# One DMA for both heads' keys and queries, and the first expert weights one unit earlier

## The chip, the cores and the metric

The kernel runs on one core of a Trainium2 chip. The metric is the device time of one execution in microseconds (us). Five engines work side by side, each through its own queue in order: PE (matmuls and transposes), DVE (elementwise work and reductions), ACT (activations and copies), POOL (elementwise work) and SP, which here only issues the DMA transfers.

## The reference

Three layers follow each other: attention, a mixture layer with one expert, and one with four.

```python
# q, k, v: (2, 8, 576, 64), f32
q_d, k_d, v_d = (t.reshape(B, H, 144, 4, D).mean(3) for t in (q, k, v))
out_up = np.repeat(softmax(q_d @ k_d.T / 8) @ v_d, 4, axis=2)     # pooled attention
scores = np.where(np.abs(i - j) < 4, q @ k.T / 8, -1e9)           # local band
out = out_up + softmax(scores) @ v
x = out.transpose(0, 2, 1, 3).reshape(1152, 512)
x = (s * np.maximum(x @ w_in, 0) ** 2 + b) @ w_out                # 512 -> 2048 -> 512
p = probs / (probs.sum(-1, keepdims=True) + 1e-9)
y = sum(p[:, e:e+1] * (np.maximum(x @ w1[e], 0) @ w2[e]) for e in range(4))   # 512 -> 1024 -> 512
```

The weights `w_in` and `w_out` of the first layer arrive as 64-bit floats, read as pairs of 32-bit words.

## The kernel before

**Attention** is cut into 16 units. Unit u covers two heads (j = u mod 4) and one of four groups of tokens (two batches, each in halves of 256 and 320 queries). The units go through a software pipeline of eight steps: iteration i runs `a_step` of unit i (transposes of keys and queries, `kT`, `qz`, `qd`), `k_step` (pooled keys, on POOL), `b_step` of unit i-1 (scores, maxima `ml` and `md`, exponentials `pl` and `pd`), `norm_step` and `v_step` of i-1, `c_step` of i-2 (transposes of the probabilities), `d_step` of i-3 (values, `ud`, `xg`) and `x_step` of i-3 (the unit's columns of x, in two parts: ACT writes the high part, POOL the low one, L717 and L719). Keys are loaded only for the first half of a batch (units 0 to 3 and 8 to 11), queries for each unit, both two iterations ahead (`load_k`, `load_q`).

**The weights** stream through `load_next`, one piece of 1 MB at a time into the pool `raw` with two buffers. A piece of the first layer is converted by `prep` in six steps: ACT takes the magnitude (L157), DVE clamps it (L161), joins the words (L167 and L175) and puts the sign on (L186), ACT makes the high part (L196), DVE the low part (L199). The last step also calls `load_next` for the next piece. The steps wait in the list `side`; `side_step` takes one, four times in an iteration. The first layer's first block has four pieces, called c0 to c3 here: c0 and c1 hold `w_in`, c2 and c3 `w_out`. The next block's first two, c4 and c5, follow. Products of the first block (L316, `psm`) are put between the attention's steps: those on x for the first group of tokens add up unit by unit.

**What sets the order.** The program is written as a list of steps, and a scheduler of the framework sets each engine's order from it, except on POOL, where the order is as written. On the chip each engine runs its queue in that order, so an instruction that waits holds up all behind it. SP issues the transfers in its own order, and a transfer waits there for its buffer and for one of eight completion counters, each of which is used again by the eighth transfer after it.

Of the kernel before, what the change touches and what calls it, by code (L numbers as in the profile page):

```python
# [8 lines left out]
F32 = mybir.dt.float32  # L9
# [13 lines left out]
def attn_moe_moe_kernel(  # L23
# [14 lines left out]
    nc = tc.nc  # L38
    B, H, S, D = q.shape
# [4 lines left out]
    TQ = 64  # L44
# [6 lines left out]
    FAC = 4  # L51
    SD = S // FAC
    ND = SD // 2
    KP = 96
    KR = S // KP
# [44 lines left out]
    def load_next():  # L100
        if not stream:
            return
        n, which, half = stream.pop(0)
        wi, wo, f0 = blocks[n]
        m = 2 if n < n_moe1 else 1
        dt = I32 if n < n_moe1 else F32
        if n < n_moe1:
            wi, wo = wi.bitcast(I32), wo.bitcast(I32)
        f0 += half * 256
        if which == 0:  # L110
            src = wi[:, f0 * m : (f0 + 256) * m].rearrange("(k p) f -> p k f", p=P)
        else:
            src = wo[f0 : f0 + 256, :].rearrange("(c p) d -> p c d", p=P)
        if n < n_moe1:
            t = rawp.tile([P, 2048], dt, tag="raw", name="raw")
        else:
            if "raw2" not in pools:
                t = rawp.tile([P, 2048], dt, tag="raw", name="raw2")
                pools["raw2"] = [t[:, :1024], t[:, 1024:]]
            t = pools["raw2"].pop(0)  # L120
            pools["raw2"].append(t)
        nc.sync.dma_start(out=t.rearrange("p (a b) -> p a b", a=src.shape[1]), in_=src)
        raw[n, which, half] = t
# [205 lines left out]
    def make_mask(t, m):  # L329
        if t == 0:  # L330
            nc.gpsimd.memset(mask, 0.0)
        off = t * TQ - window(t) if t <= MX else S - TQ - window(NTQ - 1)
        for sgn in (1, -1):
            nc.gpsimd.affine_select(
                out=mask[:, t : t + m],
                in_=mask[:, t : t + m],
                compare_op=ALU.is_ge,
                fill=NEG,
                base=FAC - 1 + sgn * off,
                pattern=[[0, m], [-sgn, W]],  # L340
                channel_multiplier=sgn,
            )
# [7 lines left out]
    def keep_warm(ps, c0, m):  # L350
        for _ in range(m if c0 < 448 else 0):
            nc.tensor.matmul(  # L352
                ps[:, c0:], idle[:, :P], idle[:, : 512 - c0], start=True, stop=True
            )
# [11 lines left out]
    def norm_probs():  # L366
        nc.vector.tensor_reduce(out=prs, in_=pr, axis=AX.X, op=ALU.add)
        nc.vector.tensor_scalar(out=prs, in0=prs, scalar1=1e-9, scalar2=None, op0=ALU.add)
        nc.vector.reciprocal(out=prs, in_=prs)
        nc.vector.tensor_tensor(  # L370
            out=pr, in0=pr, in1=prs.to_broadcast([P, NT // P, E]), op=ALU.mult
        )
# [7 lines left out]
    ap4 = rctx.enter_context(tc.tile_pool(name="att4", bufs=1, side="right"))  # L380
# [15 lines left out]
    def unit(u):  # L396
        g, j = divmod(u, NP)
        b, hf = divmod(g, HALVES)
        return g, j, b, hf

    def tiles(hf):

        return (0, CUT) if hf == 0 else (CUT, NTQ - CUT)
# [6 lines left out]
    def bank():  # L410
        return psa.tile([P, 512], F32, tag="a", name="psa")
# [14 lines left out]
    def load_k(u):  # L426
        if u < NU and unit(u)[3] == 0:
            g, j, b, hf = unit(u)
            kn = ap4.tile([KP, KR, 2, D], F32, tag="kn", name="kn", bufs=2)
            for a in range(2):  # L430
                nc.sync.dma_start(
                    out=kn[:, :, a], in_=k[b, 2 * j + a].rearrange("(p r) d -> p r d", r=KR)
                )
            loaded["k", u] = kn

    def load_q(u):
        if u < NU:
            g, j, b, hf = unit(u)
            n0, m = tiles(hf)
            gd = m * TQ // FAC  # L440
            qn = ap2.tile([MX * TQ // FAC, FAC, 2, D], F32, tag="qn", name="qn")
            for a in range(2):
                nc.sync.dma_start(
                    out=qn[:gd, :, a],
                    in_=q[b, 2 * j + a, n0 * TQ : (n0 + m) * TQ, :].rearrange(
                        "(n r) d -> n r d", r=FAC
                    ),
                )
            loaded["q", u] = qn

    def load_v(u):
# [494 lines left out]
    def l1_steps(n, g):  # L946
        hs = hidden[n, g] = []
        if n < n_moe1:
            return [lambda fc=fc: moe1_l1(n, g, fc, hs) for fc in range(FC)]

        def run(half, i):
            if i == 0:
                hidden["steps"] = moe2_l1(n, g, half, hs)
            hidden["steps"][i]()

        return [lambda half=half, i=i: run(half, i) for half in range(2) for i in range(4)]

    def l2_steps(n, g):
        if n < n_moe1:
            return [lambda dc=dc: moe1_l2(n, g, dc, hidden[n, g]) for dc in range(KD)]  # L960
        t0, m = PARTS[g]
        return [
            lambda i=i: moe2_l2(n, t0 // P + i, i * P, hidden[n, g]) for i in range(2 * m // P)
        ]
# [6 lines left out]


    load_k(0)
    load_q(0)
    make_mask(0, 1)
    make_mask(1, CUT - 1)
    load_k(1)
    load_q(1)
    keep_warm(bank(), 0, 8)
    pool_order = ExitStack()  # L980
    pool_order.enter_context(tc.manual_schedule(engines={mybir.EngineType.Pool}))
# [12 lines left out]
    for i in range(last + 1):  # L994
        if i == 1:
            make_mask(CUT, 2)
            make_mask(MX + 1, 1)
        if i == 2:
            side += prep(0, 0, 0) + prep(0, 0, 1) + prep(0, 1, 0) + prep(0, 1, 1)
        if i == NU - 1:  # L1000
            norm_probs()
        if i == NU - NP:
            rctx.close()
            pools["wx"] = ctx.enter_context(
                tc.tile_pool(name="wx", bufs=1, side="right", reuse_waits="tile")
            )
            side += prep(1, 0, 0) + prep(1, 0, 1)
        for f, lag in steps:
            u = i - lag
            if 0 <= u < NU:  # L1010

                with tc.high_priority(30) if f is a_step and u < NP else nullcontext():
                    f(u)
            if f is x_step and u >= 0 and u % NP == NP - 1:
                slots += l1_steps(0, u // NP) + l2_steps(0, u // NP)
                if u < NP:

                    for _ in range(3):
                        slots.pop(0)()
            if f in (k_step, c_step) and slots and i < last:  # L1020
                slots.pop(0)()
            if f in (b_step, k_step, c_step, v_step):
                side_step()
        load_k(i + 2)
        load_q(i + 2)
        load_v4(i)
        load_v(i)
        if i == 4:
            load_small()
        if i < 2:  # L1030
            load_next()
    pool_order.close()
    while len(slots) > 4:
# [100 lines left out]
```

## Time and profile before

| | us |
|---|---|
| median of 3 runs | 708.98 |
| lowest and highest | 701.22, 710.42 |
| the profiled execution: its time | 706.03 |
| its span on the core | 704.2 |
| PE busy in the span | 690.5 (98%) |
| DVE, ACT, POOL busy | 417.0, 341.6, 105.0 |

The attention and the first block lie in the first 154 us; behind them the products follow without a gap. Busy time of PE counts matmuls at either granted clock. The page gives the clock in tenths of full speed (2.4 GHz): 1.00 is that, 0.50 is 1.2 GHz.

### The profile page before, as it was taken

Reading aid. Unit: us, or ns where it says so; the run is one execution under the profiler, and the core shown is the slowest. Engines: PE = TensorE matmul, PEld = TensorE weight load, DVE = VectorE, ACT = ScalarE, POOL = GpSimd, SP = SyncE. Lnnn points to the kernel's source line nnn. Section 1 sums busy time; section 2 is a strip of 40 time slices with the busy share of each in tenths; the row PEclk is TensorE's granted clock in tenths of the full one; section 3 lists DMA queues with packets and bytes.
Section 4 is the critical chain, followed back from the end, with each engine's and each line's share of the span. In section 5 each row is a group of like instructions: output and inputs, shape, how many; then the busy total and the mean of one; then the engine's idle time right before and its main releaser. Section 6 shows DMA issues by size and latency. Waiting matters only on the chain.

```text
span 704.2 us, 11441 instructions
## 1 busy us (share of the span) xinstructions
PE 690.5 (98%) x4496; PEld 629.8 (89%) x4496; DVE 417.0 (59%) x759; ACT 341.6 (49%) x830; POOL 105.0 (15%) x128
## 2 busy tenths in 40 slices
PE   8799999999999999999999999999999999999997
PEld 5678888899999999999899898899898998998996
DVE  3898848869893532578443645645645556365442
ACT  3666646768695655775443424324324234233220
POOL 5320353010000200103011111201210212010000
PEclk9979959999999999999999999999999999999999
DMA  8764625323350000100120200202201112021012
GB/s 183 192 175 95 118 61 139 114 84 118 122 179 1 1 31 1 61 1 31 30 60 31 61 31 31 89 2 59 61 30 60 31 31 70 21 61 31 1 58 77
DMA packets 54549, 46.40 MB, mean 66 GB/s; under 512 B 32608, under 2 KB 43104, under 8 KB 54496
## 3 DMA queue, kind: packets, MB, share of 16 engines
q1 hardware_dynamic: 54496, 45.67, 23.3%
q8 instruction: 35, 0.57, 0.3%
q14 instruction: 18, 0.15, 0.1%
HBM read 43.31 MB, written 2.36 MB: 65 GB/s over the span
## 4 chain that ended last, share of the span: by engine, by line
PE 89%; DVE 6%; ACT 2%; DMA 1%; issue 1%; POOL 1%; SPq 0%; ACTq 0%; POOLq 0%; DVEq 0%
PE psm L316 42%; PE psx L867 25%; PE psx L316 13%; PE psa L600 2%; PE psa L688 2%; PE psa L660 2%; DMA kn<-in_k_dram 1%; PE psa L618 1%; PE psa L681 1%; PE psa L512 1%; PE psa L494 1%; DVE cv L175 1%; DVE cv L161 0%; PE psa L352 0%; ACT cv L157 0%
## 5 line engine op out<-in xcount | busy, mean ns | idle before, releaser
L316 PE MATMUL psm<-w,h 128*128 128x512 f32 x864 | 208.7, 391 | 0.0
L316 PEld LDWEIGHTS psm<-w,h 128*128 128x128 f32 x864 | 158.5, 188 | 30.0
L867 PE MATMUL psx<-x,w 128*128 128x320 f32 (+1 forms) x768 | 117.7, 296 | 0.0
L867 PEld LDWEIGHTS psx<-x,w 128*128 128x128 f32 x768 | 109.2, 189 | 1.7
L259 POOL TENSOR_TENSOR sw<-raw 128x256 f32<-128x256 f32 x32 | 30.4, 971 | 407.5 <-DMA raw<-in_moe_w_dram 268.7
L882 ACT COPY r<-psx 128x320 f32<-128x320 f32 (+1 forms) x96 | 38.0, 396 | 92.7 <-PE psx L867 92.5
L885 ACT ACTIVATE h<-r 128x320 fp32r<-128x320 f32 (+1 forms) x96 | 42.1, 444 | 83.8 <-DVE r L896 83.8
L938 DVE SCALAR_TENSOR_TENSOR acc<-psm,pr,acc 128x512 f32<-128x512 f32 x63 | 47.2, 749 | 57.8 <-PE psm L316 57.8
L867 PE MATMUL psx<-t,w 128*128 128x320 f32 (+1 forms) x448 | 80.2, 302 | 0.2 <-DVE r L896 0.2
L316 PE MATMUL psm<-x,w 128*128 128x320 f32 (+2 forms) x420 | 74.4, 325 | 4.2 <-ACT x L717 3.3
L896 DVE TENSOR_TENSOR r<-psx,r 128x320 f32<-128x320 f32 (+1 forms) x96 | 43.2, 456 | 59.0 <-PE psx L867 57.1
L316 PEld LDWEIGHTS psm<-x,w 128*128 128x128 f32 x420 | 66.7, 199 | 6.8 <-ACT x L717 3.8
L867 PEld LDWEIGHTS psx<-t,w 128*128 128x128 f32 x448 | 67.0, 188 | 4.5 <-DVE r L896 0.5
L886 DVE SCALAR_TENSOR_TENSOR h<-r,h 128x320 fp32r<-128x320 f32 (+1 forms) x96 | 47.6, 501 | 18.5 <-ACT h L885 16.4
L316 PE MATMUL psm<-h,w 128*128 128x256 f32 (+2 forms) x360 | 58.0, 306 | 0.0
L316 PE MATMUL psx<-h,w 128*128 128x384 f32 (+1 forms) x312 | 55.9, 327 | 0.0
L316 PEld LDWEIGHTS psm<-h,w 128*128 128x128 f32 x360 | 51.0, 189 | 1.9 <-issue 1.3
L316 PEld LDWEIGHTS psx<-h,w 128*128 128x128 f32 x312 | 52.0, 188 | 0.0
L316 PE MATMUL psx<-x,w 128*128 128x384 f32 (+2 forms) x252 | 43.1, 320 | 0.0
L316 PEld LDWEIGHTS psx<-x,w 128*128 128x128 f32 x252 | 40.6, 188 | 0.0
L237 DVE TENSOR_TENSOR w<-raw,w 128x1024 fp32r<-128x1024 f32 x16 | 19.5, 1224 | 25.4 <-ACT w L234 25.4
L784 DVE TENSOR_TENSOR h<-r,h 128x384 fp32r<-128x384 f32 (+2 forms) x40 | 21.6, 541 | 19.7 <-ACT h L783 18.4
(109 smaller groups left out, 894.1 us busy)
## 6 DMA issues: line engine op xcount, KB each, us to landing
raw<-in_moe_w_dram SPq DMA_DIRECT2D x32, 512.0 KB
raw<-in_moe_w_in_dram SPq DMA_DIRECT2D x8, 1024.0 KB
raw<-in_moe_w_out_dram SPq DMA_DIRECT2D x8, 1024.0 KB
kn<-in_k_dram SPq DMA_DIRECT2D x16, 144.0 KB
v<-in_v_dram SPq DMA_DIRECT2D x8, 288.0 KB
out_dram<-acc SPq DMA_DIRECT2D x9, 256.0 KB
qn<-in_q_dram SPq DMA_DIRECT2D x16, 80.0 KB
vn<-in_v_dram SPq DMA_DIRECT2D x16, 72.0 KB
```

What stands on the lines that cost most here:

```text
L237: nc.vector.tensor_tensor(out=k0[1], in0=source(), in1=f32(k0[0]), op=ALU.subtract)
L259: nc.gpsimd.tensor_tensor(out=operand(out), in0=operand(x), in1=operand(y), op=op)
L316: nc.tensor.matmul(o, stat(ps, kk), mov(pm, kk, i), start=c == 0, stop=c == len(terms) - 1)
L600: nc.tensor.matmul(ps[0][:, t * W : t * W + W], qz[:, t].rearrange("p a q -> p (a q)"), kT[:, k0 : k0 + W], start=False, stop=t == m - 1,)
L660: nc.tensor.transpose(ps[:W, n : n + width], x, ident[:width, :width])
L784: nc.vector.tensor_tensor(out=h[1], in0=r, in1=f32(h[0]), op=ALU.subtract)
L867: nc.tensor.matmul(ps, s_ap(n, half, a, w, kk), xt[x, pi][b][:, kk], start=first and c == 0, stop=c == len(terms) - 1, skip_group_check=True,)
L882: nc.scalar.copy(t, st[name])
L885: nc.scalar.activation(out=h[0][:, halves[hf]], in_=t, func=ACTF.Relu)
L886: nc.vector.scalar_tensor_tensor(out=h[1][:, halves[hf]], in0=t, scalar=0.0, in1=f32(h[0][:, halves[hf]]), op0=ALU.max, op1=ALU.subtract,)
L896: nc.vector.tensor_tensor(out=st[t], in0=st[name], in1=st[t], op=ALU.add)
L938: nc.vector.scalar_tensor_tensor(out=a, in0=ps, scalar=p_e, in1=a, op0=ALU.mult, op1=ALU.add)
```

## The change

Each pair of transfers for the two heads' keys becomes one, and so does each pair for the queries; the keys get a third buffer. The first piece of the weights is issued before the loop, behind the keys and queries of units 0 and 1 and ahead of those of unit 2; the second at the end of iteration 0, where the first was; the third and later ones come, as before, when a piece is converted. The conversion starts in iteration 1 in place of iteration 2.

```diff
--- before.py
+++ after.py
@@ -426,11 +426,10 @@
     def load_k(u):
         if u < NU and unit(u)[3] == 0:
             g, j, b, hf = unit(u)
-            kn = ap4.tile([KP, KR, 2, D], F32, tag="kn", name="kn", bufs=2)
-            for a in range(2):
-                nc.sync.dma_start(
-                    out=kn[:, :, a], in_=k[b, 2 * j + a].rearrange("(p r) d -> p r d", r=KR)
-                )
+            kn = ap4.tile([KP, KR, 2, D], F32, tag="kn", name="kn", bufs=3)
+            nc.sync.dma_start(
+                out=kn, in_=k[b, 2 * j : 2 * j + 2].rearrange("a (p r) d -> p r a d", r=KR)
+            )
             loaded["k", u] = kn
 
     def load_q(u):
@@ -439,13 +438,12 @@
             n0, m = tiles(hf)
             gd = m * TQ // FAC
             qn = ap2.tile([MX * TQ // FAC, FAC, 2, D], F32, tag="qn", name="qn")
-            for a in range(2):
-                nc.sync.dma_start(
-                    out=qn[:gd, :, a],
-                    in_=q[b, 2 * j + a, n0 * TQ : (n0 + m) * TQ, :].rearrange(
-                        "(n r) d -> n r d", r=FAC
-                    ),
-                )
+            nc.sync.dma_start(
+                out=qn[:gd],
+                in_=q[b, 2 * j : 2 * j + 2, n0 * TQ : (n0 + m) * TQ, :].rearrange(
+                    "a (n r) d -> n r a d", r=FAC
+                ),
+            )
             loaded["q", u] = qn
 
     def load_v(u):
@@ -976,6 +974,7 @@
     make_mask(1, CUT - 1)
     load_k(1)
     load_q(1)
+    load_next()
     keep_warm(bank(), 0, 8)
     pool_order = ExitStack()
     pool_order.enter_context(tc.manual_schedule(engines={mybir.EngineType.Pool}))
@@ -995,7 +994,7 @@
         if i == 1:
             make_mask(CUT, 2)
             make_mask(MX + 1, 1)
-        if i == 2:
+        if i == 1:
             side += prep(0, 0, 0) + prep(0, 0, 1) + prep(0, 1, 0) + prep(0, 1, 1)
         if i == NU - 1:
             norm_probs()
@@ -1027,7 +1026,7 @@
         load_v(i)
         if i == 4:
             load_small()
-        if i < 2:
+        if i == 0:
             load_next()
     pool_order.close()
     while len(slots) > 4:
```

How this moves instructions is seen on two engines. **SP, from its first transfer on** (kn is a unit's keys, qn its queries, v4 and vn its values, raw a piece of the weights). Before:

```order
L431 DMA kn_118<-in_k_dram 96x6x64 x2
L443 DMA qn_121<-in_q_dram 64x4x64 x2
L431 DMA kn_137<-in_k_dram 96x6x64 x2
L443 DMA qn_140<-in_q_dram 64x4x64 x2
L418 DMA v4_196<-in_v_dram 72x4x256
L458 DMA vn_198<-in_v_dram 72x2x64
L431 DMA kn_190<-in_k_dram 96x6x64 x2
L443 DMA qn_193<-in_q_dram 64x4x64 x2
L465 DMA vn_198<-in_v_dram 72x3x64 x2
L122 DMA raw_202<-in_moe_w_in_dram 128x4x512
```

Now:

```order
L430 DMA kn_118<-in_k_dram 96x12x64
L441 DMA qn_120<-in_q_dram 64x8x64
L430 DMA kn_135<-in_k_dram 96x12x64
L441 DMA qn_137<-in_q_dram 64x8x64
L122 DMA raw_139<-in_moe_w_in_dram 128x4x512
L430 DMA kn_188<-in_k_dram 96x12x64
L441 DMA qn_190<-in_q_dram 64x8x64
L418 DMA v4_192<-in_v_dram 72x4x256
L456 DMA vn_194<-in_v_dram 72x2x64
L463 DMA vn_194<-in_v_dram 72x3x64 x2
L122 DMA raw_198<-in_moe_w_in_dram 128x4x512
```

The 16 transfers ahead of the first piece of the weights have become four, and the keys and queries of unit 2 stand behind that piece; the second piece, which stood behind unit 3's loads, stands ahead of them.

**DVE, units 0 and 1** (ml and md are negated maxima, qz and qd a unit's queries, cv the piece in conversion). Before, from unit 0's `ml` to unit 1's `pl` scaling there is no conversion:

```order
L608 TENSOR_REDUCE ml_217<-psa_220 128x4
L526 TENSOR_SCALAR qz1_109<-psa_253 64x4x64
L620 TENSOR_REDUCE md_219<-psa_220 128x1
L533 TENSOR_REDUCE qd1_111<-psa_253 64x64 x2
L608 TENSOR_REDUCE ml_300<-psa_303 128x4
L633 TENSOR_SCALAR sum0_106<-sum0_106 128x7
L634 RECIPROCAL sum0_106<-sum0_106 128x7
L635 TENSOR_TENSOR pl_216<-pl_216,sum0_106 128x288
```

Now the first piece stands between, its first step ahead of unit 0's `ml`:

```order
L606 TENSOR_REDUCE ml_221<-psa_224 128x4
L524 TENSOR_SCALAR qz1_109<-psa_259 64x4x64
L531 TENSOR_REDUCE qd1_111<-psa_259 64x64
L618 TENSOR_REDUCE md_223<-psa_224 128x1
L531 TENSOR_REDUCE qd1_111<-psa_259 64x64
L167 TENSOR_SCALAR cv_238<-cv_238 128x1024
L175 SCALAR_TENSOR_TENSOR cv_238<-raw_139,cv_238 128x1024
L631 TENSOR_SCALAR sum0_106<-sum0_106 128x7
L606 TENSOR_REDUCE ml_298<-psa_301 128x4
L632 RECIPROCAL sum0_106<-sum0_106 128x7
L186 SCALAR_TENSOR_TENSOR cv_238<-raw_139,cv_238 128x1024
L633 TENSOR_TENSOR pl_220<-pl_220,sum0_106 128x288
```

**DVE, from unit 8's maxima to `xg` of unit 6** (cv_1431 and cv_1552 are c4 and c5 in the program before, cv_1529 is c5 in the new one). Before:

```order
L175 SCALAR_TENSOR_TENSOR cv_1431<-raw_819,cv_1431 128x1024
L161 TENSOR_SCALAR cv_1552<-cv_1552 128x1024
L186 SCALAR_TENSOR_TENSOR cv_1431<-raw_819,cv_1431 128x1024
L633 TENSOR_SCALAR sum0_106<-sum0_106 128x7
L167 TENSOR_SCALAR cv_1552<-cv_1552 128x1024
L634 RECIPROCAL sum0_106<-sum0_106 128x7
L175 SCALAR_TENSOR_TENSOR cv_1552<-raw_927,cv_1552 128x1024
L526 TENSOR_SCALAR qz1_109<-psa_1108 64x4x64
L533 TENSOR_REDUCE qd1_111<-psa_1108 64x64 x2
L697 TENSOR_SCALAR ud_1150<-psa_1135 128x80
L635 TENSOR_TENSOR pl_1079<-pl_1079,sum0_106 128x288
L705 TENSOR_TENSOR xg_1152<-psa_1135,ud_1150 128x320
```

Now:

```order
L175 SCALAR_TENSOR_TENSOR cv_1529<-raw_814,cv_1529 128x1024
L633 TENSOR_TENSOR pl_936<-pl_936,sum1_107 128x360
L636 TENSOR_TENSOR pd_938<-pd_938,sum1_107 80x288
L618 TENSOR_REDUCE md_1064<-psa_1065 128x1
L524 TENSOR_SCALAR qz1_109<-psa_1090 64x4x64
L531 TENSOR_REDUCE qd1_111<-psa_1090 64x64 x2
L695 TENSOR_SCALAR ud_1132<-psa_1117 128x80
L199 TENSOR_TENSOR w01_1388<-cv_1409,w00_1387 128x1024
L703 TENSOR_TENSOR xg_1134<-psa_1117,ud_1132 128x320
```

Between unit 8's `md` and unit 9's `qz` stood five steps of conversion, and none now; one step of c5 stands ahead of unit 7's scaling, and the low part of c4 (L199) has come ahead of `xg`.

## Rows read from the trace of the kernel before

**Rows 1.** Windows by stage: busy us of each engine (instructions), PEclk, DMA share, GB/s.

```profile
0.00:22.00 22.00, 18.68 (x125) 13.04 (x126) 9.42 (x28) 10.10 (x33) 10.20 (x26) 1.00 0.87 191
22.00:46.00 24.00, 20.94 (x184) 16.48 (x181) 21.76 (x38) 14.43 (x51) 9.77 (x10) 0.86 0.73 179
290.00:704.00 414.00, 410.10 (x2447) 372.77 (x2445) 222.60 (x394) 155.63 (x339) 51.12 (x57) 1.00 0.13 41
```

**Rows 2.** Windows: the three stretches at the lower granted clock.

```profile
31.90:38.70 6.80, 6.80 (x48) 5.43 (x48) 4.80 (x8) 3.97 (x14) 1.80 (x2) 0.50 0.50 107
48.90:55.60 6.70, 6.70 (x49) 5.92 (x48) 4.88 (x15) 4.44 (x19) 0.78 (x1) 0.50 0.93 233
86.30:103.50 17.20, 16.02 (x83) 13.93 (x84) 9.13 (x23) 6.94 (x30) 8.69 (x8) 0.50 0.26 58
```

**Rows 3.** Waits of PE, 0 to 140 us: total us, times, longest.

```profile
PE psm L316 <- ACT x L717: 3.3, 2, 2.0
```

**Rows 4.** Timeline of SP's DMA queue: start, us, what [idle before].

```profile
0.74 1.38 SPq L431 DMA_DIRECT2D kn<-in_k_dram  x2
...
6.15 0.60 SPq L418 DMA_DIRECT2D v<-in_v_dram  x1
...
11.00 0.41 SPq L122 DMA_DIRECT2D raw<-in_moe_w_in_dram  x1
```

**Rows 5.** DMA issues of the page: sizes of one load.

```profile
raw<-in_moe_w_in_dram SPq DMA_DIRECT2D x8, 1024.0 KB
...
kn<-in_k_dram SPq DMA_DIRECT2D x16, 144.0 KB
```

**Rows 6.** Chain that ended last, its first loads: start, us, what.

```profile
1.51 3.63 DMA kn<-in_k_dram
...
7.94 4.09 DMA kn<-in_k_dram
```

**Rows 7.** Windows: the DMA engines while small pieces, then while large ones are moved.

```profile
2.00:8.00 6.00, 5.44 (x32) 2.89 (x31) 0.52 (x2) 1.25 (x4) 2.20 (x6) 1.00 0.68 152
13.00:16.00 3.00, 3.00 (x22) 2.32 (x21) 0.89 (x3) 2.37 (x12) 0.35 (x2) 1.00 1.01 351
```

**Rows 8.** Timeline of ACT: start, us, what [idle before <- releaser].

```profile
11.81 0.38 ACT L524 ACTIVATE qz<-psa 64x256 f32<-64x256 f32 x1 [1.98 <-PE psa L352]
...
19.70 1.14 ACT L157 ACTIVATE cv<-raw 128x1024 f32<-128x1024 f32 x1
```

**Rows 9.** Timeline of DVE, 11 to 30 us.

```profile
11.42 0.46 DVE L608 TENSOR_REDUCE ml<-psa 128x4 f32<-128x288 f32 x1 [1.99 <-PE psa L600]
...
16.23 0.46 DVE L608 TENSOR_REDUCE ml<-psa 128x4 f32<-128x288 f32 x1 [2.33 <-PE psa L600]
...
28.73 1.22 DVE L199 TENSOR_TENSOR w<-cv,w 128x1024 fp32r<-128x1024 f32 x1
29.87 0.42 DVE L705 TENSOR_TENSOR xg<-psa,ud 128x256 f32<-128x256 f32 x1
```

**Rows 10.** Timeline of DVE: L161 twice.

```profile
33.94 0.69 DVE L161 TENSOR_SCALAR cv<-cv 128x1024 f32<-128x1024 f32 x1 [1.88 <-ACT cv L157]
...
42.40 1.45 DVE L161 TENSOR_SCALAR cv<-cv 128x1024 f32<-128x1024 f32 x1
```

**Rows 11.** Timeline of POOL, 41 us.

```profile
41.03 2.26 POOL L474 TENSOR_TENSOR v<-v 72x512 f32<-72x512 f32 x1
```

**Rows 12.** Timeline of PE, 47 us.

```profile
46.83 1.34 PE L600 MATMUL psa<-kT,qz 128*128 128x72 f32 x10 [0.68 <-DVE qz L526]
```

**Rows 13.** Timeline of DVE, 78 to 86 us.

```profile
78.74 1.21 DVE L175 SCALAR_TENSOR_TENSOR cv<-raw,cv 128x1024 int32<-128x1024 int32 x1
...
82.40 1.57 DVE L175 SCALAR_TENSOR_TENSOR cv<-raw,cv 128x1024 int32<-128x1024 int32 x1
...
85.35 0.24 DVE L697 TENSOR_SCALAR ud<-psa 128x80 f32<-128x80 f32 x1
```

**Rows 14.** Timeline of PE, 87 us.

```profile
86.90 0.90 PE L316 MATMUL psm<-x,w 128*128 128x320 f32 x2 [1.31 <-ACT x L717]
```

## The prediction

> **What bounds the kernel now.** I read the busy time by stage first. From 290 us on, PE is busy 410.1 of 414 us [rows 1], and the products look the same from 154 us; no edit touches an instruction there, so what can change lies in the first 154 us. In the first 22 us DVE is busy for only 9.4 us and POOL for 10.2; from 22 to 46 us DVE is busy 21.8 of 24 and PE 20.9 [rows 1]: the reader is to see DVE as the pace there and PE behind it.
>
> Second, the granted clock. It is 0.50, the 1.2 GHz level, in three stretches: 6.8, 6.7 and 17.2 us long [rows 2]. PE is busy throughout the first two and 16.0 us of the third, so at full clock that work would take 3.4, 3.4 and 8.0 us less. What PE did before each: it had waited 0.68 us for unit 5's queries at 46.8 us, two us before the second [rows 12], and 1.31 us for x of unit 6 until 86.9, where the third begins [rows 14]. The waits for x on ACT come to 3.3 us, two in number, the longest 2.0 [rows 3]: so the other is that of 2.0, and it ends where unit 0's x is written (its `xg` at 29.87 [rows 9]), just ahead of the first stretch.
>
> Third, SP's queue and the chain: the chain begins with keys that land (3.63 us from 1.51, 4.09 from 7.94 [rows 6]), and SP issues without a pause, two loads in 1.38 us at the start, up to the first piece of the weights at 11.00 [rows 4].
>
> **The change, part by part** (against the profiled execution, 706.0 us, 2.9 below the median of the runs, 709.0).
>
> *One load for two.* Unit 0's keys: now the second half starts at 1.51 and takes 3.63, landed at 5.14 [rows 6]. With one load the first bytes go 0.77 us earlier (issue at 0.74), but the other 144 KB follow in the same transfer [rows 5]; at 152 GB/s and a busy share of 0.68 [rows 7] the engines' full rate for these pieces is 152/0.68 = 224 GB/s (estimate), so 0.66 us. Gain between 0 (issue takes as long as two) and 0.77; the values' load, one transfer of the same 288 KB, is issued in 0.60 us [rows 4], nearer to one than to two, so I take 0.3, below the middle because the bytes stay. Later merged loads shorten SP's queue, which is not what is waited for after 20 us: nothing.
> The Trainium skill (DMA: Bandwidth & Descriptors, Anatomy of one DMA) fits a transfer as about 2.0 us plus its bytes at 436 GB/s; by that the merged keys would land near 4.0 and gain 1.1 us (estimate). The trace disagrees: by the same fit 144 KB take 2.3 us, and 3.63 were measured [rows 6].
>
> *The first piece ahead of unit 2's keys.* SP's four loads end about 3.4 us (four of 0.6 to 0.7), and the piece follows. Bytes ahead of it: 2 x 288 + 2 x 128 KB (unit 0's and 1's queries are 64 KB each half, by 64 rows of 1 KB) = 0.85 MB, 3.8 us at 224 GB/s from 2.0; then 1.05 MB at 351 GB/s [rows 7], 3.0 us: landed at 8.8. If SP needs as long for a merged load as for two, the issue is at 6.15 and it lands 5 us later, as it does now (issued 11.00, the fast bytes over at 16 [rows 4, 7]): 11.2. I take 10. Unit 2's keys, 0.30 MB, come 1.3 us behind: 10.1 to 12.5 against 12.03 now [rows 6]. Cost 0 (from -0.2 to +0.5): they are wanted no sooner than unit 1's `qz`, at 11.81 [rows 8].
>
> *The conversion in units 0 and 1.* ACT's L157 (1.14 us) now stands ahead of the second half of unit 1's keys; ACT idles 1.98 us before 11.81 [rows 8], which hides it if the piece lands by 10.2. If the piece lands at 11.2, ACT is 1.0 late. Behind L157 DVE's L161 (0.69 to 1.45 [rows 10]) stands ahead of unit 0's `ml`, now at 11.42 [rows 9]: 10 + 1.14 + 0.69 = 11.83, so +0.4 (0 to +2.4, with 11.2 and 1.45). Queued behind `ml` are unit 1's `qz`, then `md` and the exponentials. L167 (0.7) and L175 (1.21) fit the 2.33 us that DVE idles before 16.23 [rows 9, 13]. L186 and L199 (1.2 each) do not fit; they stand ahead of unit 0's scaling and unit 2's `ml`, +0.8 of the 2.4, since PE and ACT are late there too. Against that, L199 of the piece in turn, 1.22 us, now stands ahead of unit 0's `xg` [rows 9] and moves behind it: -1.2. Together up to x of unit 0: -0.4 + 0.4 = 0 (-1.2 to +3.2).
> The Trainium skill (SBUF — State Buffer, Who interferes with whom) says that a DVE operation with two inputs in SBUF, or in a two-port mode, and a POOL operation lock each other out of a shared port. The trace agrees: L161 took 0.69 us alone and 1.45 at 42.40, beside POOL's addition from 41.03 to 43.29 [rows 10, 11]. It speaks against the change, since POOL is busy 10.2 of the first 22 us [rows 1]; if L161 and L167 both meet POOL the sum below rises by some 1.2 us.
>
> *The later pieces.* Four steps per iteration stay, so c1 takes c0's place, c2 c1's, and DVE has as much work from 22 to 54 us as before: no gain from the sum of it. But the places shift. Unit 5's `qz` no longer has c2 ahead of it, so PE's wait of 0.68 [rows 12] goes: -0.7. Unit 6's `ud` at 85.35 stood behind five steps from 78.74 to 83.97 [rows 13], 5.2 us; none is left there, one L199 (1.2) stands before `xg`. So PE's wait of 1.31 for that x [rows 14], with the low part behind it, shrinks to about 0.6 with it: -0.7, and the following wait for POOL's part of it, 0.6, goes too: -1.3 (0 to -1.9). Late next is POOL's own part of x.
>
> Sum: -0.3 + 0 - 0.7 - 1.3 = -2.3, so 703.7 us with the clock as it is.
>
> **The rivals.**
> 1. *The long low stretch goes with the wait.* For: the clock falls where PE waited 1.31 us [rows 2, 14], and that wait halves. Against: the 0.68 us wait preceded a fall too [rows 2, 12]. Price: 17.2 us hold 16.0 us of PE work at half clock, 8.0 less. 703.7 - 8.0 = 695.7; with one of the short ones too, 692.3.
> 2. *Nothing arrives at the end.* PE is bound by its own work from 47 to 85 us, the early gains only shift its waits, and c5's L175 and c4's L199 make x of unit 6 as late as now. 706, from 705 to 707.
> 3. *Slower: the piece lands too late.* ACT and DVE stand in order behind it. It decides from 10.2 us on; at 11.2 us it costs up to 2.4 at `ml`, and a PE wait of that length is longer than that of 1.31 us, which preceded a low stretch, so one of 6.7 us is added, 3.4. 706 + 2.4 + 3.4 - 1.3 = 710.5. For: it is the only place where a transfer is put ahead of attention's own in ACT's and DVE's order. Against: SP's queue gives it a start 5 us before it is needed, and the engines moved 351 GB/s for large rows [rows 7].
> 4. *The edit does not do what it says*: a merged load is issued as slowly as two. Then the start gains nothing and the piece comes at 11.2, which is rival 3.
>
> **How the numbers follow.** My forecast has 0.42; rival 1 0.28; rival 2 0.17; rivals 3 and 4 together 0.13. The predicted time is that of the forecast, rounded to 703.5 us; its own range is 701.5 to 705.5 (the bounds of the early conversion and of x of unit 6, half of them). The range takes in rival 1 from 694 and rival 3 to 711; left out are its upper tail and the half of the combination with a second stretch, together under 0.2. A measurement of this kernel tells about 2% from no change, 14 us: under 694.8 or over 723.2 against the median. Faster by that is only rival 1 with luck at a second stretch, or about half of it: 0.14. Slower needs two or three new low stretches: 0.02. Within: 0.84.
>
> **What will show it.** In the changed profile: unit 0's keys landed between 4.4 and 5.1 us; L157 first at about 10 us, and ACT's wait before it (over 1 us means rival 3); `ml` of unit 0 before 12.2; PE's wait at unit 5's scores gone; its wait for x of unit 6 under 0.7 us; and the three low stretches, which decide between 704 and 695. I am wrong if a low stretch appears in the first 25 us, or if one stands between 154 and 290 us where none is now.

## The result: 0.7% slower, and the profile after

The change takes 710.03 us (median of 20 runs, 704.35 to 714.11) against 703.09 for the kernel before (20 runs): ratio 1.0073, 95% interval 1.0049 to 1.0096. Run again beside other kernels it was 1.0073 (1.0036 to 1.0110). That is less than the 2% that the prediction named, but both intervals leave out 1. The forecast was 703.5, faster than the kernel before, whose median was 708.98 over three runs then and is 703.09 over twenty; the change is slower. The time itself lies inside the stated range, on the side of rival 3. All ratios leave out executions more than 1.5% above the fastest of their own kernel, which in the sets of the experiments are 1 to 10 of the kernel before and none of the change; with every execution counted, the mean of change_again lies 0.4% above that of the kernel before (2.7 us of span), and the means of moves_only and early_load_late_conv 0.4% and 0.3%. The profiled execution took 710.17 us, with a span of 708.4 against 704.2.

Windows by stage, after the change, as [rows 1]:

```profile
0.00:22.00 22.00, 18.25 (x96) 12.79 (x96) 10.60 (x22) 7.26 (x21) 10.15 (x25) 0.79 0.99 200
22.00:46.00 24.00, 20.36 (x158) 15.96 (x157) 19.29 (x39) 13.41 (x47) 8.24 (x7) 0.77 0.49 130
290.00:704.00 414.00, 413.81 (x2477) 376.88 (x2476) 224.70 (x398) 158.33 (x345) 53.70 (x60) 1.00 0.13 42
```

PE is hardly less busy in the first 46 us (38.6 against 39.6 us), but its clock, 1.00 and 0.86 before, is 0.79 and 0.77. Windows of the stretches at the lower level, and last the place of the third one of [rows 2]:

```profile
12.90:33.10 20.20, 16.91 (x77) 13.11 (x77) 18.09 (x30) 10.62 (x42) 8.78 (x9) 0.50 0.85 195
46.90:63.50 16.60, 15.87 (x90) 12.80 (x91) 9.02 (x21) 8.44 (x35) 3.59 (x4) 0.50 0.52 118
70.90:74.00 3.10, 3.10 (x16) 2.94 (x15) 3.10 (x8) 3.10 (x17) 0.00 (x0) 0.50 1.25 225
86.30:103.50 17.20, 16.82 (x167) 15.10 (x165) 16.39 (x37) 10.78 (x39) 8.82 (x9) 1.00 0.35 78
```

The first three hold 35.9 us of PE work at half clock, so by the prediction's way of counting they cost 17.9 us; those before held 29.5, so 14.8 [rows 2]. The difference, 3.2 us, is most of the 4.2 us of span. These are upper bounds: in the first stretch DVE is busy for 18.09 of 20.20 us, so a faster PE would have waited for it in part. The long stretch at 86 us is gone, and a longer one stands at the start. What precedes it is the first piece of the weights. Chain that ended last:

```profile
0.74 0.74 SPq L430
...
2.98 0.97 SPq L441
...
4.00 8.30 DMA raw<-in_moe_w_in_dram
12.30 0.02 issue
12.32 0.03 ACT cv L157
```

Timeline of ACT, then of DVE, then of PE, all of the change:

```profile
8.78 0.47 ACT L498 ACTIVATE kT<-psa 128x288 f32<-128x288 f32 x1 [0.63 <-PE psa L352]
12.32 1.12 ACT L157 ACTIVATE cv<-raw 128x1024 f32<-128x1024 f32 x1 [3.07 <-DMA raw<-in_moe_w_in_dram]
13.34 0.46 ACT L498 ACTIVATE kT<-psa 128x288 f32<-128x288 f32 x1
```

```profile
13.47 0.69 DVE L161 TENSOR_SCALAR cv<-cv 128x1024 f32<-128x1024 f32 x1 [3.98 <-ACT cv L157]
14.20 0.46 DVE L606 TENSOR_REDUCE ml<-psa 128x4 f32<-128x288 f32 x1
...
16.46 1.80 DVE L167 TENSOR_SCALAR cv<-cv 128x1024 int32<-128x1024 int32 x1
...
28.95 0.68 DVE L161 TENSOR_SCALAR cv<-cv 128x1024 f32<-128x1024 f32 x1
29.55 0.30 DVE L618 TENSOR_REDUCE md<-psa 128x1 f32<-128x144 f32 x1
29.76 0.68 DVE L167 TENSOR_SCALAR cv<-cv 128x1024 int32<-128x1024 int32 x1
30.48 1.23 DVE L175 SCALAR_TENSOR_TENSOR cv<-raw,cv 128x1024 int32<-128x1024 int32 x1
31.74 1.23 DVE L186 SCALAR_TENSOR_TENSOR cv<-raw,cv 128x1024 int32<-128x1024 int32 x1
...
35.26 0.42 DVE L703 TENSOR_TENSOR xg<-psa,ud 128x256 f32<-128x256 f32 x1
```

```profile
12.04 0.29 PE L589 MATMUL psa<-mask,identb 64*128 64x288 bf16 x1
14.80 0.82 PE L610 MATMUL psa<-kd,qd 128*128 128x144 f32 x2 [2.47 <-POOL tk L552]
```

Read from the last line back: PE stands still for 2.47 us; POOL's `tk` needs `kT`, which ACT writes only at 13.34, behind L157, which waited 3.07 us for the piece. Unit 0's `ml` is at 14.20 instead of 11.42 [rows 9], the clock is down from 12.9 us, and `xg` of unit 0 comes at 35.26 instead of 29.87.

The loss is larger on the way than at the end. `xg` of unit 0 is 5.4 us later than before, that of unit 3 13.8, that of unit 5 13.0, and then that of unit 9 only 4.0 (116.66 against 112.69) and that of unit 15 3.7: between 75 and 117 us the change wins back 9.

### The profile page after: what moved, and what is told of

It is laid out like the page before. It is cut to its first block, busy times and chain, and to the rows that moved or that the text cites. A ratio compares the mean times of both kernels' runs of the same rounds, so it can differ in the third digit from the quotient of the medians.

```text
span 708.4 us, 11406 instructions
## 1 busy us (share of the span) xinstructions
PE 693.4 (98%) x4496; PEld 631.5 (89%) x4496; DVE 422.9 (60%) x759; ACT 341.3 (48%) x830; POOL 106.6 (15%) x128
## 4 chain that ended last, share of the span: by engine, by line
PE 89%; DVE 4%; issue 2%; ACT 2%; POOL 1%; DMA 1%; SPq 0%; POOLq 0%; ACTq 0%; DVEq 0%
PE psm L316 41%; PE psx L865 25%; PE psx L316 13%; PE psa L598 2%; PE psa L686 2%; PE psa L658 2%; DMA raw<-in_moe_w_in_dram 1%; PE psa L352 1%; PE psa L616 1%; PE psa L679 1%; POOL x L717 1%; PE psa L510 1%; DVE ts L837 0%; DVE h L775 0%; PE psa L492 0%
## 5 line engine op out<-in xcount | busy, mean ns | idle before, releaser
L259 POOL TENSOR_TENSOR sw<-raw 128x256 f32<-128x256 f32 x32 | 30.5, 972 | 407.4 <-DMA raw<-in_moe_w_dram 221.2
L884 DVE SCALAR_TENSOR_TENSOR h<-r,h 128x320 fp32r<-128x320 f32 (+1 forms) x96 | 48.1, 506 | 18.5 <-ACT h L883 16.4
```

Of the source, the lines that this page charges most:

```text
L259: nc.gpsimd.tensor_tensor(out=operand(out), in0=operand(x), in1=operand(y), op=op)
L884: nc.vector.scalar_tensor_tensor(out=h[1][:, halves[hf]], in0=t, scalar=0.0, in1=f32(h[0][:, halves[hf]]), op0=ALU.max, op1=ALU.subtract,)
```

## The experiments

Each run reports its span and mean granted clock, so span x clock is called its work part and span x (1 - clock) its clock part. "Gaps" are the waits of PE, by its timeline, that end between 12 and 24 us of the profiled execution; "first low" is where the first stretch at 0.50 begins there (to half a us, except in the first two rows). Ratios are to the kernel before, with 95% intervals; parts are means over the runs compared.

| kernel | ratio | clock part | work part | gaps | first low |
|---|---|---|---|---|---|
| before | 1 | 13.5 to 16.4 | 688.6 to 689.6 | 1.57 | 31.9 |
| the change | 1.0073 (1.0049, 1.0096) | 18.3 | 689.8 | 3.22 | 12.9 |
| change_again | 1.0073 (1.0036, 1.0110) | 17.9 | 690.0 | 4.25 | 21 |
| moves_only | 1.0061 (1.0021, 1.0101) | 19.4 | 689.1 | 4.37 | 14.5 |
| early_load_late_conv | 1.0058 (1.0021, 1.0095) | 18.1 | 690.0 | 2.25 | 20 |
| merge_only | 0.9984 (0.9934, 1.0033) | 15.9 | 687.8 | 1.08 | 17.5 |
| load_only | 0.9995 (0.9953, 1.0038) | 11.8 | 691.9 | 1.60 | 30.5 |
| c0_behind | 1.0013 (0.9972, 1.0054) | 14.7 | 691.6 | 2.40 | 19 |
| c1_behind_x | 1.0104 (1.0038, 1.0170) | 19.3 | 692.0 | 2.96 | 21 |
| c1_behind_x_fast | 0.9984 (0.9949, 1.0019) | 12.6 | 691.3 | 3.18 | 21.5 |
| late_pieces_sooner | 1.0061 (1.0033, 1.0089) | 21.2 | 688.7 | 1.34 | 31.5 |
| one_step_sooner | 0.9985 (0.9950, 1.0021) | 17.1 | 687.0 | 1.34 | 28 |
| fill_3 | 1.0070 (1.0025, 1.0115) | 24.2 | 685.3 | 4.14 | 17.5 |
| fill_6 | 0.9957 (0.9929, 0.9986) | 6.6 | 693.2 | 0 | 38 |
| fill_8 | 0.9980 (0.9940, 1.0020) | 8.4 | 695.1 | 0 | 35.5 |
| before_fill_6 | 0.9956 (0.9929, 0.9984) | 7.3 | 693.6 | 0 | 40.5 |
| change_fill_6 | 0.9977 (0.9944, 1.0009) | 8.7 | 694.0 | 2.68 | 33.5 |
| one_step_fill_6 | 1.0012 (0.9982, 1.0041) | 13.9 | 690.7 | 0 | 29 |
| c1_fast_fill_6 | 1.0042 (1.0011, 1.0073) | 13.7 | 692.9 | 1.72 | 24.5 |

c1_behind_x has 6 executions, the others 12 or 13. Against before the change's work part is 0.2 to 1.4 us larger, its clock part 2.4 to 4.8: more of the loss is clock than work. The two rows of the change come from different sets; a difference of two clock parts is uncertain by some 3 us either way. Against load_only, run in the same set as change_again, the clock part is 6.1 us larger and the work part 1.9 smaller.

### Which part of the edit

**merge_only**: the two loads merged, `load_next()` and the conversion where they were.

> Merged loads alone: the loads of keys and queries are merged and keys have three buffers, load_next() and the conversion stay where they were in the kernel before. Theory 1 (the early first piece stalls ACT and DVE, PE idles 2.5 us and the clock is low for 20 us behind it): as before, ratio to before 0.997 to 1.003; no wait of ACT for raw ahead of unit 0's ml, ml of unit 0 at 11.0 to 11.6 us (11.42 before, 14.20 after the change), no clock of 0.50 before 30 us. Theory 2 (the merged loads themselves, by their order in the DMA queue, cost the time): 1.005 to 1.010, unit 0's or unit 1's keys later than before. Theory 3 (the DVE work put into the first units costs it, beside POOL): as before, like theory 1.

The ratio is as theories 1 and 3 have it, and theory 2 falls. Against the text of theory 1, `ml` of unit 0 is at 12.22, and a low stretch of 3.5 us did begin at 17.5 us.

**moves_only**: the other half, with two loads as before.

```diff
     load_q(1)
+    load_next()
...
-        if i == 2:
+        if i == 1:
             side += prep(0, 0, 0) + ...
...
-        if i < 2:
+        if i == 0:
             load_next()
```

> The moves alone: load_next() ahead of unit 2's keys and the conversion from the second unit on, with two loads for keys and for queries as before and two buffers for keys. Theory 1: the piece is issued at about 6.15 us (where unit 2's keys are issued now) and lands at 13 or later, so ACT's wait for raw is 3 us or more, ml of unit 0 at 14.5 or later, a stretch at clock 0.50 begins between 12 and 16 us; ratio to before 1.005 to 1.015, as the change or worse. Theory 2: as before, 0.997 to 1.003. Theory 3: as the change, 1.005 to 1.010, even if ml of unit 0 came at 11.5.

The loss is in the moves. The piece lands no later than with merged loads (ACT's L157 starts at 12.23 here, 12.32 in the change), though SP issues it at 6.15 instead of 4.00 us: so the time of issue alone does not set the landing. Theory 1 had it land at 13 or later and `ml` of unit 0 at 14.5 or later; `ml` is at 14.11.

**early_load_late_conv**: the change with `if i == 2:` for the conversion.

> The change, but the conversion steps of the pieces begin with the third unit as before; the load of the first piece stays early, and so do L157 and L161 of it in ACT's and DVE's order; L167, L175, L186 and L199 of it and every later piece's load and steps stand as late as in the kernel before. Theory 1: the wait is the same (ml of unit 0 at 13.8 to 14.6, clock 0.50 from about 13 us on), and what the change wins back at 86 to 106 us is not won: 1.008 to 1.020 of before, no faster than the change. Theory 2: as the change, 1.005 to 1.010. Theory 3: nearly as before, under 1.004, since most of the DVE work is back where it was.

The same loss, but by another path than I wrote. The edit did not take the steps back: L167 of the first piece stands at 15.81, where it was at 23.86 before, so this run does not tell the early load from the early steps. ACT did not wait for the piece here, as it came to L157 only at 11.08; unit 1's first `kT`, ahead of it, started at 10.73 instead of 8.78. Timeline of ACT, then of DVE, then of PE:

```profile
11.08 1.13 ACT L157 ACTIVATE cv<-raw 128x1024 f32<-128x1024 f32 x1
```

```profile
15.81 1.13 DVE L167 TENSOR_SCALAR cv<-cv 128x1024 int32<-128x1024 int32 x1
16.97 1.64 DVE L175 SCALAR_TENSOR_TENSOR cv<-raw,cv 128x1024 int32<-128x1024 int32 x1
18.53 0.63 DVE L631 TENSOR_SCALAR sum<-sum 128x7 f32<-128x7 f32 x1
```

```profile
19.80 0.69 PE L610 MATMUL psa<-kd,qd 128*128 128x144 f32 x2 [1.89 <-DVE sum L632]
```

PE's gap is that of unit 1's scores, behind L167 and L175 on DVE, and the clock falls at 20 us, right behind it. In change_again both gaps are there (1.21 us at 13.5, 1.73 at 19.1, 1.31 at 20.9; ACT's wait for the piece is 1.81). So the wait for the piece varies, from none to 3.3 us, and theory 1 was too narrow: conversion steps, waiting or working, stand ahead of unit 0's and 1's scores where the gaps open.

**load_only**: merged loads, the first piece's load early, every conversion step where it was. The edit against merge_only, with cuts:

```diff
     load_q(1)
+    load_next()
...
-        if i < 2:
+        if i == 1:
             load_next()
...
-            nc.scalar.activation(out=f, in_=words()[1].bitcast(F32), func=ACTF.Abs)
+            with tc.issue_after(st0["act"]) if (n, which, half) == (0, 0, 0) else nullcontext():
+                nc.scalar.activation(out=f, in_=words()[1].bitcast(F32), func=ACTF.Abs)
...
+            if u == 1:
+                st0["act"] = r.ins     # unit 1's last exponential
```

> Merged loads, and the load of the first piece ahead of unit 2's keys; every conversion step where it was before (L157 of the first piece is ordered behind unit 1's exponentials on ACT, the steps begin with the third unit, the second piece's load stays behind the second unit's loads). Over its runs span x granted clock is called the work part and span x (1 - granted clock) the clock part: 689.6 and 13.5 us before, 689.8 and 18.3 after the change. Theory 1 (the wait of ACT and DVE for the piece, and the low clock behind it): no wait, so 0.996 to 1.003 of before, ml of unit 0 at 11.0 to 12.2, clock part 11 to 16. Rival 4 (the megabyte put ahead of unit 2's keys and the first values delays those, whatever ACT does): 1.004 to 1.010, PE waits for kn or for values of units 0 to 2 that add up to 1 us or more.

No loss is seen: the megabyte in the queue ahead of unit 2's keys costs nothing by itself that shows, and rival 4 of the expectation falls.

### Taking the steps out of the way

**c0_behind**: the change with L157 of the first piece ordered behind unit 0's exponentials.

> The change, with one order added: ACT's L157 (its first instruction on the first piece) waits in ACT's order until unit 0's exponentials are issued, and DVE's steps on the piece follow it; loads and all else as in the change. Theory 1: ACT no longer waits for raw ahead of unit 1's keys, ml of unit 0 at 11.0 to 11.8 us, PE's wait of 2.5 us for unit 0's difference scores gone, no stretch at clock 0.50 that begins at 12 to 14 us; what the change wins at 86 to 106 us stays, so 0.982 to 0.995 of the change (4 to 13 us) and 0.985 to 1.000 of before. Theory 2: as the change, 1.005 to 1.010 of before. Theory 3: as the change or within 0.3% of it, since the same DVE work stands in the same units, one step later.

The clock part fell by 3.6 us, as theory 1 has it, but the work part rose by 1.8. By the ratios (1.0013 against 1.0073) it is 0.6% faster than the change, at the lower end of the 4 to 13 us that I expected; by the mean spans, 706.2 against 708.1, it is 1.9 us. `ml` of unit 0 is back at 11.68, yet `xg` of unit 0 comes at 34.03. Timeline of DVE:

```profile
26.50 1.23 DVE L163 TENSOR_SCALAR cv<-cv 128x1024 f32<-128x1024 f32 x1
...
28.45 0.68 DVE L169 TENSOR_SCALAR cv<-cv 128x1024 int32<-128x1024 int32 x1
29.16 1.23 DVE L177 SCALAR_TENSOR_TENSOR cv<-raw,cv 128x1024 int32<-128x1024 int32 x1
30.43 1.57 DVE L188 SCALAR_TENSOR_TENSOR cv<-raw,cv 128x1024 int32<-128x1024 int32 x1
32.03 0.43 DVE L526 TENSOR_SCALAR qz<-psa 64x256 f32<-64x256 f32 x1
```

The second piece's steps, 4.7 us, stand ahead of `xg` of unit 0; before the change none of them did.

**c1_behind_x**: besides, the second piece's steps begin behind x of unit 0 (`side += prep(0, 0, 1) + ...` moved behind `x_step` of iteration 3, and its L157 ordered behind L715 of unit 0).

> The change, with L157 of the first piece ordered behind unit 0's exponentials (as in c0_behind) and the second piece's steps begun only behind x of unit 0 (ordered on ACT behind L715 of unit 0; that is two of the four steps of an iteration later than before the change, and all later pieces with it). Theory 1 with rival 3 (DVE work ahead of xg of unit 0 costs the rest): both causes gone, xg of unit 0 at 28.5 to 31 (29.87 before, 35.26 after, 34.03 in c0_behind), span x clock 688 to 690.5, ratio 0.990 to 1.003 of before; the later pieces being later, a wait for x of unit 6 or for w may grow by 1 us. Theory 1 alone (DVE work costs nothing): as c0_behind, 1.000 to 1.004, xg of unit 0 still after 33.

A miss: 1.0104. `xg` of unit 0 is at 31.87, not 28.5 to 31, and the later pieces come half an iteration later than before.

**c1_behind_x_fast**: the same with one more step in iterations 4 to 7.

```diff
-            if f in (b_step, k_step, c_step, v_step):
+            if f in (b_step, k_step, c_step, v_step) or (f is d_step and 3 < i < 8):
                 side_step()
```

> c1_behind_x with one conversion step more in each of four iterations (the fifth to the eighth), which takes the later pieces to where the change has them or earlier. If the earlier conversion of pieces 4 and 5 is what wins back 9 us between 75 and 106 us in the change (no low stretch at 86 to 103 us, PE no longer waiting for x of unit 6), that comes here on top of c1_behind_x: 0.982 to 0.995 of before, lateness against before falling by 5 to 9 us between xg of unit 5 and xg of unit 9. If not (the win there was only that the early loss left more to do later), as c1_behind_x within 0.3%.

That took back the loss of c1_behind_x, so the later pieces' place matters (mean spans of 703.8 against 711.4 us); but it is not faster than before by more than the noise. Where no engine waits for the piece, no gain of the early load shows.

**late_pieces_sooner** and **one_step_sooner**: merge_only with the extra step in iterations 3 to 7, and 4 to 7.

> merge_only (loads and first piece as before the change) with a fifth conversion step in the fourth to eighth iteration: the first two pieces stand where they stood before, the pieces behind them come sooner, so that the second-half pieces' steps stand ahead of unit 5's queries and fewer between those and xg of unit 6 (2 instead of 6). This takes the prediction's last step (x of unit 6) by itself. Theory (what the change wins back between 75 and 106 us is the wait for x of unit 6 and the low clock behind it, and comes from the later pieces' place): that wait of PE under 0.7 us, no stretch at 0.50 that begins at 84 to 90 us, 0.984 to 0.997 of before. Rival (low stretches come and go, the place of the later pieces does not set them): 0.997 to 1.004 of before, another low stretch elsewhere, clock part within 2 us of before's.

> merge_only with a fifth conversion step in the fifth to eighth iteration, which moves only one step of the late pieces ahead of unit 5's queries; all before that as in merge_only. Theory: a part of late_pieces_sooner, x of unit 6 about 1.2 us earlier (83.7 to 84.7 instead of 85.9), 0.990 to 1.000 of before. Rival: as merge_only, 0.997 to 1.003.

The theory of late_pieces_sooner falls. The wait for x of unit 6 and the stretch behind it went, as forecast, but windows of its profile show what came instead:

```profile
42.20:72.80 30.60, 30.02 (x166) 24.94 (x167) 21.09 (x40) 13.41 (x47) 3.44 (x4) 0.50 0.67 154
103.60:107.00 3.40, 3.40 (x16) 3.28 (x16) 2.58 (x6) 0.73 (x2) 2.72 (x3) 0.52 0.50 84
```

Its work part is that of before and its clock part 5 us larger: the same loss as the change's with neither its wait nor its early steps. one_step_sooner moved little and changed nothing, as its rival said.

**change_again**: the change itself.

> The change itself, beside the others on one chip. All theories: 1.004 to 1.010 of before. Theory 1: the clock part 16 to 21 us against 12 to 15 of before, the work part within 1.5 us of before's; if waits alone cost it, the clock parts would be equal and the work part 4 to 5 us more.

### The clock by itself

The kernel already runs four matmuls on an idle tile behind each group of transposes and each unit's value products (`keep_warm`). The next three are merge_only with another number.

```diff
-    fill = [4 if u < NP else 0 for u in range(NU)]
+    fill = [6 if u < NP else 0 for u in range(NU)]      # 3, 6, 8
```

> merge_only with 3 instead of 4 matmuls on the idle tile at each of the kernel's places for them (units 0 to 7). 'Clock part' is span x (1 - granted clock), 'work part' span x granted clock, means over the runs. Theory A (the clock part is set by how full PE is between the scores of the first units): clock part 3 us or more above before's, work part 0 to 4 us lower, since 45 matmuls of some 0.1 us are missing. Theory B (the low stretches are set by something else, the fillers only cost PE time): clock part within 2 us of before's, ratio 0.993 to 1.000.

> merge_only with 6 instead of 4 idle matmuls at each place (units 0 to 7; the order of the first units' steps on DVE shifts with them). Theory A: clock part 4 us or more below before's, work part up by 2 to 6 us, ratio 0.990 to 1.003. Theory B: clock part within 2 us of before's, ratio 1.002 to 1.010.

> merge_only with 8 instead of 4 idle matmuls at each place. Theory A: clock part under 7 us (half of before's or less), work part up by 5 to 12 us, ratio 0.990 to 1.006. Theory B: clock part within 3 us of before's, ratio 1.005 to 1.018.

(The program has 20 such places, all in units 0 to 3: one matmul more at each is 20 matmuls. The expectations miscount them.) Theory A holds, but for fill_8's last bit: clock parts of 24.2, 15.9, 6.6 and 8.4 us with 3, 4, 6 and 8, while the work part climbs from 685.3 to 695.1. Of these 6 is best, and the kernel is 0.43% faster than before. Windows of 0 to 154 us, first of fill_3, then of fill_6:

```profile
0.00:154.00 154.00, 139.91 (x1088) 116.72 (x1089) 106.63 (x236) 85.49 (x296) 43.62 (x61) 0.81 0.57 126
```

```profile
0.00:154.00 154.00, 144.43 (x1286) 123.17 (x1287) 118.87 (x252) 95.14 (x326) 51.03 (x64) 0.93 0.59 133
```

**change_fill_6**, **before_fill_6**, **one_step_fill_6** and **c1_fast_fill_6** put six into the change, the kernel before, one_step_sooner and c1_behind_x_fast.

> The change with 6 instead of 4 idle matmuls at each place of units 0 to 3 (there are 18 such places; the first two DVE steps on the first piece stand ahead of ml of unit 0 in this order, so the wait for the piece is there as in the change or 0.5 us longer). If the change's loss is the low clock behind PE's wait: clock part 5 to 9 us (18 in the change), work part 692 to 695, 0.993 to 1.000 of before, as fill_6 within 2 us. If the wait costs by itself (units late, idle PE): clock part as low, but 3 us or more above fill_6's 699.8 in span.

> The kernel before with 6 instead of 4 idle matmuls, two loads for each pair of heads as before; the order on all engines but SP is that of fill_6. Tells what the merged loads are worth where the clock is mostly high: by the prediction's first step 0.3 us (0 to 0.8) more than fill_6, so 0.9950 to 0.9985 of before; if merging is worth more, 1.000 or above.

> fill_6 with the fifth conversion step of one_step_sooner in the fifth to eighth iteration. one_step_sooner had a work part 1.5 us below before's; if that holds with the higher clock, span 697 to 699.5 (fill_6: 699.8), 0.989 to 0.996 of before; if it was chance, as fill_6.

> c1_behind_x_fast (the early load kept, no engine waiting for it, the later pieces hastened) with 6 idle matmuls. If its work part stays 2 to 3 us above before's plus the idle matmuls' 4 us: 700 to 703 in span, 0.994 to 1.000 of before; the early load is then worth nothing even where it costs no wait. If the early load is worth something once the clock is up, under 699 (0.992).

With six, the change's clock part falls from about 18 to 8.7 us, and its span from 708 to 702.7. The wait is still there; timeline of PE in change_fill_6:

```profile
11.99 0.83 PE L352 MATMUL psa<-idle 128*128 128x256 bf16 x6
...
14.56 0.48 PE L610 MATMUL psa<-kd,qd 128*128 128x144 f32 x2 [1.51 <-POOL tk L552]
```

but the first low stretch begins at 33.5 instead of 12.9 us. Timeline of DVE, `xg` of unit 0, in change_fill_6 and then in before_fill_6:

```profile
35.87 0.41 DVE L703 TENSOR_TENSOR xg<-psa,ud 128x256 f32<-128x256 f32 x1
```

```profile
28.39 0.42 DVE L705 TENSOR_TENSOR xg<-psa,ud 128x256 f32<-128x256 f32 x1
```

Unit 0 is 7.5 us late here, more than in the change, and yet only 1.7 us remain at the end (702.7 against 701.0), of which 1.4 are clock part; without the added matmuls the loss was 3.9 to 5.0. So the early steps' lateness by itself costs little where the clock is mostly up, and most of their harm seems to go through the clock; the two losses differ by little more than their noise, about 2 us. before_fill_6 equals fill_6 (0.9956, 0.9957): no gain of the merged loads shows with the clock up either. The last two missed: both have clock parts near 14 us in spite of the idle matmuls. before_fill_6 and fill_6 beat both kernels; no kernel with the early load did so beyond its noise.

**What is shown and what is open.** Shown: the loss comes with conversion begun ahead of unit 0's exponentials (the change, change_again, moves_only and early_load_late_conv) and not with merged loads or the early load alone; idle matmuls in units 0 to 3 move the clock part by up to 18 us, and the change's with it. Argued: that the loss goes mainly through the clock. The change against load_only and the loss left in change_fill_6 say so, but moves_only and early_load_late_conv have 1.3 and 2.2 us more work part than merge_only besides their larger clock part. Nor is such an early start the only way to a loss of this size: late_pieces_sooner and c1_behind_x have one without it. Where the gaps listed are large the first low stretch comes early, except in change_fill_6, and where they are small it comes later, except in merge_only; that is a pattern of single executions, not a rule, and that the gaps make the clock fall is not shown. Open: why a stretch lasts as long as it does (late_pieces_sooner: 30.6 us with PE busy for 30.0), and so why one order of the later pieces costs 5 us of clock and another none. No kernel here has the change's exact order and PE's gap filled, since each added matmul also moved the order on DVE and ACT.

## Why the prediction failed, step by step

**One load for two**: right in the issue, but the gain was not seen. SP issues unit 0's keys in 0.74 us against 1.38 [rows 4], so rival 4's premise was wrong; PE's first transpose of keys stands at 4.88 instead of 5.28, but at 5.32 in change_again, and ACT's first `kT` in the change at 6.21 instead of 6.14. Forecast 0.3; neither merge_only nor before_fill_6 shows any gain.

**The first piece lands at 10 us**: too early, and this is where the loss begins in the profiled execution. The piece was issued at 4.00, 0.6 us later than I had it, and landed at 12.3, outside my 8.8 to 11.2; in change_again it landed at 11.0, inside. I let the bytes ahead of it pass at 224 GB/s and then the piece alone at 351 [rows 7]. Windows of the change:

```profile
4.00:8.00 4.00, 3.91 (x26) 2.45 (x25) 0.00 (x0) 1.17 (x3) 0.61 (x1) 1.00 1.15 192
8.00:10.00 2.00, 2.00 (x18) 1.67 (x18) 1.27 (x3) 0.62 (x2) 1.47 (x6) 1.00 1.03 362
10.00:13.00 3.00, 2.34 (x14) 1.55 (x14) 0.00 (x0) 0.68 (x1) 0.00 (x0) 0.95 1.21 181
```

Packets of the change by size, from 4 to 8 us, from 8 to 10 and from 10 to 13:

```profile
DMA packets 1985, 0.77 MB, mean 192 GB/s; under 512 B 1834, under 2 KB 1834, under 8 KB 1985
```

```profile
DMA packets 489, 0.72 MB, mean 362 GB/s; under 512 B 153, under 2 KB 153, under 8 KB 489
```

```profile
DMA packets 1659, 0.54 MB, mean 181 GB/s; under 512 B 1526, under 2 KB 1634, under 8 KB 1659
```

The piece is 512 rows of 2 KB, the packets that are under 8 KB and not under 2 KB. From 4 to 8 us 151 of them were moved and from 8 to 10 us 336, so the bulk came nearly as I had it; the last 25 trailed behind 10 us among 1634 smaller packets of attention's loads, and ACT's wait for the piece ended at 12.3. I had let the transfers behind the piece in SP's order, issued from 4.84 us on, count for nothing. That they held up the last rows is likely, but not shown.

The Trainium skill (DMA: Bandwidth & Descriptors, Anatomy of one DMA — SWDGE (gpsimd) path) fits a transfer that POOL issues as about 2.0 us plus its bytes at 436 GB/s; for 1 MB that is an estimate of 4.4 us. The piece, issued by SP with other transfers on either side, took 8.30 us, so the fit does not carry over to it; the prediction used it on SP's loads without saying so.

**The early conversion**: this is the step that failed in every execution of the change. I put it at 0 up to x of unit 0, between -1.2 and +3.2, and the sum left the clock as it was. `xg` of unit 0 came 5.4 us later (3.9 in change_again), outside the bound, and the clock was down for 20.2 us from 12.9 us on, where the first low stretch before was 6.8 us long and began at 31.9 [rows 2]. `ml` of unit 0 moved by 2.8 us, where rival 3 said up to 2.4 and I took 0.4. Two terms were wrong behind it. Four steps of the second piece, 3.8 us from 28.95 on, came to stand ahead of `xg` of unit 0, and the sum did not have them: it only took L199 away. And I counted L167 and L175 as free in DVE's idle time; L167 took 1.80 us at 16.46, beside POOL's work on the values (16.45 to 18.84), and in each of the four executions with early steps PE then waited for DVE, between 19 and 23.2 us, for 0.75 to 3.0 us in all.

The Trainium skill (SBUF — State Buffer, Who interferes with whom) says that a DVE operation in a two-port mode and a POOL operation lock each other out; the trace agrees, 1.80 us against 0.68 for L167 at 29.76, where POOL is idle.

**The later pieces**: right where it looked. The wait for x of unit 6 went from 1.31 us [rows 14] to 0.38, and the long stretch behind it with it: the 8.0 us at which rival 1 priced that stretch lie within the 9 won back. Unit 5's wait for `qz` [rows 12] moved to unit 4, 0.72 us at 43.72. But late_pieces_sooner shows that this gain can't be counted on: the same repair elsewhere brought a low stretch of 30.6 us.

**Rival 3** was the mechanism in the profiled execution, a late piece with ACT and DVE in order behind it, and its price, 710.5, met the 710.2 of the profile by luck, since two errors cancelled: I added one low stretch of 3.4 us, and there were three, counted at 17.9 us, in place of those before, at 14.8; against it stood the 8 us of rival 1, which I had kept apart from rival 3. It got 0.13 together with rival 4 because I took the piece's landing as nearly sure. The sign that I had named for being wrong, a low stretch in the first 25 us, came at 12.9 us; merge_only has one at 17.5 us and no loss, so the sign alone tells little.

## What to carry to other kernels

That work on weights which arrive by DMA seems to fit into idle time is no reason to put it ahead of the critical operations of an in-order engine: here the same piece, issued at 4.00 and 4.06 us, landed at 12.3 us in one execution and at 11.0 in another. Before pricing an early wait in microseconds, read what it does to PE's clock, by splitting each run into span x clock and span x (1 - clock); here the change's work part was 0.2 to 1.4 us above before's and its clock part 2.4 to 4.8. And try the number of idle matmuls first: two more at 20 places were worth 0.4%, and no move of a load here gained anything clear of noise.

## What was not expected of the hardware

PE stays at 1.2 GHz for 30.6 us while it is busy for 30.0 of them (late_pieces_sooner). The DMA engines' rate falls from 362 to 181 GB/s within three microseconds, with a busy share above 1 in both; 336 of 489 packets are rows of 2 KB in the first stretch and 25 of 1659 in the second. ACT's wait for the same megabyte, issued at 4.00, 4.06 and 4.13 us, was 3.07, 1.81 and 0 us in three executions (the change, change_again and early_load_late_conv); in the last ACT came to it later.
